# Layer-norm variance with eps out of the aggregation, one more unit by seven block products, and new instruction orders, in a two-layer long-convolution and SwiGLU kernel

## The chip, the cores and the metric

The kernel runs on one core of a Trainium2 chip. The core has a matrix engine (TensorE, PE in the profile, with its weight loads as PEld), a vector engine (VectorE, DVE), an activation engine (ScalarE, ACT), a general engine (GpSimd, POOL), a queue engine that here only issues DMAs (SyncE, SP), and 16 DMA engines. The metric is the device time of one execution in microseconds; lower is better. A fraction of a per cent is the scale of this case.

## The reference, cut to what matters

Two blocks, A and B, are applied twice, each as a residual on the layer-normed x of 2048 rows by 512 columns:

```python
def _layernorm(x, axis=-1, eps=1e-5):
    m = jnp.mean(x, axis=axis, keepdims=True)
    v = jnp.var(x, axis=axis, keepdims=True)
    return (x - m) / jnp.sqrt(v + eps)
...
x = A_q
x = x + _A_ref(_layernorm(x, axis=-1), A_k, A_v, A_shift_k, A_ssm_k, A_ssm_D)
x = x + _B_ref(_layernorm(x, axis=-1), B_w_gate, B_w_up, B_w_down)
x = x + _A_ref(_layernorm(x, axis=-1), A_k, A_v, A_shift_k, A_ssm_k, A_ssm_D)
x = x + _B_ref(_layernorm(x, axis=-1), B_w_gate, B_w_up, B_w_down)
```

Block A computes y = causal long convolution over the 2048 rows of (short convolution of k, times v) with the kernel ssm_k, plus a skip term, and returns q * y, where q is the normed x. The convolution doesn't depend on x, so y is computed once and used by both layers. Block B is (silu(x @ w_gate) * (x @ w_up)) @ w_down, with weights of 512 x 1792, 512 x 1792 and 1792 x 512.

## The kernel before, in words

**Tiling.** The rows are cut into 4 chunks (c = 0 to 3) of 512 rows, four rows to each of 128 partitions; a chunk has two halves (h = 0, 1) of two rows per partition. A *unit* (l, c, h) is block B of layer l on one half of one chunk, 256 rows. There are 16 units. The stretch ahead of a unit, `prologue(l, c, h)` (line 926), norms x (`apply_norm`), multiplies by y, adds to x, takes the second layer norm's statistics, writes the normed rows z, and turns them by a DMA transpose (line 940) into zT, which the unit's matmuls read.

**A unit** (`ffn`, line 1085) has 14 column tiles of 128 in groups of 4, 4, 4 and 2. For each group TensorE makes gate and up products into the four PSUM banks of ring "pf", ScalarE takes them out with Silu and a copy (lines 1072 and 1073, or 1132 and 1136), VectorE multiplies them, and in the row-wise form (`by_rows`) a DMA transpose (line 1081) turns the result. Then the down product (line 1159) accumulates over all 14 tiles: 28 matmuls of 512 columns per unit into two banks of ring "pd". ScalarE copies these two banks into `dn` (line 1201) and VectorE adds `dn` to x (line 1204).

**Seven products.** For units named in `STRASSEN` a number of groups takes another way: `seven` (line 1004) makes sums of blocks of the left operand on VectorE (tile `cb`, three instructions per group, lines 1013 to 1017) and does the 2x2 block product in seven products of 256 columns (line 1034) in place of eight, into four banks (two of "pd", two of "pc"). `weight_sums` (line 981) makes the sums of the blocks of w_down once, in five VectorE instructions (lines 994 and 998). `add_seven` (line 1038) takes four banks out and adds them to x in five VectorE instructions. Before, the four units of chunk 3 take it.

**The convolution** is done by Fourier blocks per chunk: transposes of ssm_k, forward products with ScalarE evacuation (line 466), butterflies on VectorE (lines 587 to 604), spectral products `product` (lines 700 to 714, 2048 elements per partition in the large ones) and the `inverse` of chunk c (line 728), whose rows y that chunk's prologue reads. The work of `conv(c)` must be over before unit (0, c, 0) starts.

**Layer-norm statistics** come in two ways. `ln_stats` (line 851) uses VectorE: `bn_stats` gives two triples (count, mean, sum of squares about it) for each row of 512, `bn_aggr` joins them into mean and variance, a third VectorE instruction (line 859) adds eps, and GpSimd raises the result to the power -0.5 (line 861). `ln_stats_act` (line 867) uses ScalarE: a copy with an accumulated sum, a mean, a square with an accumulated sum, and GpSimd's power (line 887).

**Order.** No scheduler decides. Every instruction group is recorded as an operation with its engine, a cost in microseconds and the operations that it depends on; the list `ORDER` holds for each operation its place in the one sequence, and each engine's queue is that sequence cut down to its own operations. `Plan.order` (line 200) also walks the sequence with the given costs to pick the slot of each ring buffer (the one that comes free first). All transposing DMAs stand in SP's single queue with the loads. An engine takes its queue strictly in order, so an instruction whose operand is late holds back all that stands behind it on its engine.

Of the kernel before, what the change touches and what calls it, by code (L numbers as in the profile page):

```python
# [9 lines left out]
P = 128  # L10
# [20 lines left out]
STRASSEN = {(0, 3, 0): 4, (0, 3, 1): 4, (1, 3, 0): 4, (1, 3, 1): 2}  # L31
# [88 lines left out]
]  # L120
R = 4

NS = 8
# [21 lines left out]
class Plan:  # L147
# [52 lines left out]
    def order(self, table):  # L200
# [14 lines left out]
        for o in seq:  # L215
# [26 lines left out]
            if o.late:  # L242
# [5 lines left out]
                elif gap[1] > o.start + 0.03:  # L248
                    settle(gap[0])
                    pend = None  # L250
# [1218 lines left out]
```

## Time and profile before

| what | value |
|---|---|
| median of three runs | 340.92 us (340.49 to 341.29) |
| the profiled execution | 340.95 us, of which 339.2 us span |
| granted TensorE clock | 0.998 |
| PE busy | 332.2 us |
| DVE busy | 305.4 us |
| ACT busy | 257.8 us |
| POOL busy | 41.1 us |
| SP | 150 of its DMA issues in the trace |

How to read it: the span runs from the first to the last profiled instruction; the execution's own time is 1.75 us longer. Busy time is the union of an engine's instructions; matmul durations overlap their successors, so the spacing of matmuls in the timeline (0.216 us for 512 columns, 0.109 us for 256) is what a matmul costs, not its mean duration. The same holds in smaller measure for VectorE: a 2048-element product lasts 1.22 us and the next instruction starts after 1.135 us. In the chain of waits a line is a start, a length, and the work that the chain ran through. A timeline line ends with the idle time ahead of the instruction and what ended it.

### The profile page before, as it was taken

The page shows a single profiled execution, that of the slowest core. Times are in us where ns is not written, and L with a number is a line of the kernel's source. Part 1 is how long each engine was busy: PE and PEld are TensorE (multiplying, and loading weights), DVE is VectorE, ACT ScalarE, POOL GpSimd, SP SyncE. Part 2 cuts the span into 40 slices and gives each one's busy share as a digit, 9 for nine tenths or more (in the row PEclk, how much of TensorE's full clock was granted, in tenths as well). Part 3 has the DMA queues.
Part 4 walks back from the last instruction along what each step waited for, and adds up shares of the span by engine and source line. Part 5 has one row for each costly group of instructions (what it writes and reads, how often), then busy time and mean ns, then how long its engine had stood idle before and what let it go on. Part 6 is the DMA issues. An engine that isn't in the chain of part 4 may idle for free.

```text
span 339.2 us, 5867 instructions
## 1 busy us (share of the span) xinstructions
PE 332.2 (98%) x2119; PEld 201.9 (60%) x2151; DVE 305.4 (90%) x552; ACT 257.8 (76%) x514; POOL 41.1 (12%) x46
## 2 busy tenths in 40 slices
PE   8999999999999999999999999999999999999996
PEld 6647864644454564654445555645445487867884
DVE  7999999999999999999999999999999866987464
ACT  6899999988987467877899994869575465657463
POOL 4010110303110400103010200111201000100000
PEclk9999999999999999999999999999999999999999
DMA  7999403312643458341323245431414140213201
GB/s 287 322 312 354 59 15 79 62 31 48 140 108 77 98 123 161 75 111 31 63 48 77 46 80 129 115 37 32 89 11 94 28 92 2 49 47 73 55 0 64
DMA packets 77992, 31.59 MB, mean 93 GB/s; under 512 B 69765, under 2 KB 75786, under 8 KB 77962
## 3 DMA queue, kind: packets, MB, share of 16 engines
q1 hardware_dynamic: 77808, 31.13, 39.5%
q8 instruction: 17, 0.28, 0.4%
q14 instruction: 13, 0.11, 0.1%
q10 hardware_dynamic: 154, 0.07, 0.1%
HBM read 12.33 MB, written 2.10 MB: 43 GB/s over the span
## 4 chain that ended last, share of the span: by engine, by line
PE 83%; ACT 6%; DVE 5%; DMA 4%; issue 1%; POOL 1%; SPq 0%; ACTq 0%
PE pf L358 51%; PE pd L1159 18%; PE ps L358 6%; PE ps L1034 6%; DMA zT<-z 2%; DMA kn<-in_A_k_dram 1%; PE ps L844 1%; ACT H L466 1%; ACT X L466 1%; PE ps L505 1%; DVE bnst L856 1%; DVE m L587 1%; ACT jk L881 1%; ACT jk L875 1%; ACT hs L534 1%
## 5 line engine op out<-in xcount | busy, mean ns | idle before, releaser
L358 PEld LDWEIGHTS <-zT 128*128 128x128 bf16 x528 | 51.4, 98 | 61.1 <-DMA zT<-z 1.4
L358 PE MATMUL pf<-wu_sb,zT 128*128 128x512 bf16 x258 | 64.8, 379 | 0.4
L358 PE MATMUL pf<-wg_sb,zT 128*128 128x512 bf16 x256 | 63.6, 379 | 0.6 <-DMA zT<-z 0.3
L1159 PE MATMUL pd<-wd_sb,sg 128*128 128x512 bf16 x217 | 53.4, 379 | 0.5 <-DMA sg<-hr 0.2
L861 POOL TENSOR_TENSOR rstd<-ve,nhalf 128x2 f32<-128x2 f32 x24 | 27.9, 1165 | 206.4 <-DVE ve L859 206.4
L1072 ACT ACTIVATE sg<-pf 128x512 bf16<-128x512 f32 x66 | 38.9, 605 | 11.9 <-PE pf L358 11.4
L1073 ACT CAST hr<-pf 128x512 bf16<-128x512 f32 x66 | 38.5, 591 | 11.8 <-PE pf L358 11.0
L358 PE MATMUL pf<-zT,wg_sb 128*128 128x256 bf16 x368 | 46.7, 273 | 0.1
L358 PE MATMUL pf<-zT,wu_sb 128*128 128x256 bf16 x368 | 45.9, 273 | 0.0
L358 PEld LDWEIGHTS <-wg_sb 128*128 128x128 bf16 x368 | 35.9, 98 | 8.4
L358 PEld LDWEIGHTS <-wu_sb 128*128 128x128 bf16 x368 | 36.0, 98 | 7.3
L1159 PEld LDWEIGHTS <-sg 128*128 128x128 bf16 x224 | 21.7, 98 | 24.2 <-DMA sg<-hr 0.9
L1132 ACT ACTIVATE sg<-pf 128x512 bf16<-128x512 f32 x46 | 27.5, 608 | 8.1 <-PE pf L358 8.0
L856 DVE BATCH_NORM_STATS2 bnst<-xc 128x6 f32<-128x512 bf16 x48 | 31.4, 684 | 0.5
L1136 ACT CAST ht<-pf 128x512 bf16<-128x512 f32 x46 | 26.7, 591 | 5.7 <-PE pf L358 5.5
L1159 PE MATMUL pd<-wd_sb,ht 128*128 128x512 bf16 (+1 forms) x125 | 30.2, 369 | 0.3
L1139 DVE TENSOR_TENSOR ht<-ht,sg 128x512 bf16<-128x512 bf16 (+1 forms) x31 | 16.9, 548 | 8.5 <-ACT ht L1136 5.0
L700 DVE TENSOR_TENSOR t<-X,G 128x2048 bf16<-128x2048 bf16 x18 | 21.9, 1217 | 0.0
L704 DVE TENSOR_TENSOR t<-X,G 128x2048 bf16<-128x2048 bf16 x18 | 21.9, 1217 | 0.0
L1201 ACT CAST dn<-pd 128x512 bf16<-128x512 f32 x24 | 14.1, 594 | 10.2 <-PE pd L1159 7.6
L466 ACT ACTIVATE X<-ps 128x512 bf16<-128x512 f32 x32 | 19.1, 613 | 3.5 <-PE ps L358 3.1
L1079 DVE TENSOR_TENSOR hr<-hr,sg 128x1024 bf16<-128x1024 bf16 x27 | 18.5, 685 | 2.4 <-ACT hr L1073 1.6
(139 smaller groups left out, 506.8 us busy)
## 6 DMA issues: line engine op xcount, KB each, us to landing
hn<-in_A_ssm_k_dram SPq DMA_DIRECT2D x4, 512.0 KB, 3.9
vt<-in_A_v_dram SPq DMA_DIRECT2D x4, 512.0 KB, 6.5
xc<-in_A_q_dram SPq DMA_DIRECT2D x4, 512.0 KB, 6.2
out_dram<-xc SPq DMA_DIRECT2D x15, 128.0 KB, 1.8
wg_sb<-in_B_w_gate_dram SPq DMA_DIRECT2D x1, 1792.0 KB
wu_sb<-in_B_w_up_dram SPq DMA_DIRECT2D x1, 1792.0 KB, 7.5
wd_sb<-in_B_w_down_dram SPq DMA_DIRECT2D x1, 1280.0 KB, 11.2
sg<-hr SPq DMA_TRANSPOSE x66, 2.5
```

Source lines behind the costliest of these rows:

```text
L358: nc.tensor.matmul(o, lhsT=lhsT, rhs=rhs, start=(n == 0), stop=(n == len(terms) - 1))
L466: add("ACT", act(D), lambda: nc.scalar.activation(out=view(), in_=ps.t[:], func=ACT.Copy, scale=scale), r=[ps], w=[(buf, keys)], conv=conv)
L700: dve(n * D, lambda t1=t1, part=part: nc.vector.tensor_mul(out=t1.t[:], in0=x.t[:, sl, 0, :], in1=g.t[:, sl, part, :]), [(x, key(slots, (0 ...
L704: dve(n * D, lambda t2=t2, part=part: nc.vector.tensor_mul(out=t2.t[:], in0=x.t[:, sl, 1, :], in1=g.t[:, sl, 1 - part, :]), [(x, key(slots ...
L856: add("DVE", 0.6, lambda st=st, i=i: nc.vector.bn_stats(out=st.t[:], in_=xs[c].t[:, i, :]), r=[(xs[c], (i,))], w=[st])
L861: add("POOL", pw, lambda: nc.gpsimd.tensor_tensor(out=rstd.t[:], in0=ve.t[:], in1=nhalf.t[:].to_broadcast((P, n)), op=ALU.pow), r=[ve, nha ...
L1034: nc.tensor.matmul(bank.t[:, half_ * C:(half_ + 1) * C], lhsT=lhsT(i), rhs=rhs(i), start=(first and i == 0 and half_ == 0), stop=(last and ...
L1072: add("ACT", act(D), lambda ps=ps, dst=dst, o=o, which=which: nc.scalar.activation(out=rows(dst, o), in_=ps.t[:], func=ACT.Silu) if which ...
L1073: out=rows(dst, o), in_=ps.t[:], func=ACT.Silu) if which == "g" else nc.scalar.copy(out=rows(dst, o), in_=ps.t[:]),
L1132: add("ACT", act(D), lambda ps=ps, o=o, sg=sg: nc.scalar.activation(out=sg.t[:, o:o + 2, :], in_=ps.t[:], func=ACT.Silu), r=[ps], w=[(sg, ...
L1136: add("ACT", act(D), lambda ps=ps, o=o, ht=ht: nc.scalar.copy(out=ht.t[:, o:o + 2, :], in_=ps.t[:]), r=[ps], w=[(ht, (o // 2,))], due=(uni ...
L1159: nc.tensor.matmul((pds[o] if not cs.start else pds[HP]).t[:, cs], lhsT=ht.tiles(q, o), rhs=wt["d"].t[:, ft, cs], start=(ft == std0 and no ...
```

## The change

1. `ln_stats` no longer adds eps in an instruction of its own. The statistics go into a constant buffer `bst` with six slots of nine numbers: two triples from `bn_stats`, and a third triple (0, 0, eps x 512) that two GpSimd memsets write once. `bn_aggr` joins all three, so that its variance already holds eps, and GpSimd's power reads it from `mv` with a stride. The 24 instructions of line 859 are gone.
2. Unit (1, 2, 1) is added to `STRASSEN` with all four groups. `weight_sums` is recorded ahead of that unit instead of ahead of (0, 3, 0).
3. The inverse of chunk 3 uses PSUM ring "pf" in place of "pc" (`I_RING`), since `seven` of (1, 2, 1) takes the "pc" banks.
4. For (1, 0, 0) the row sums come from the two copies of `dn` in unit (0, 0, 0), with an accumulator, and from the mean that the statistics before had given; one VectorE instruction joins them. Two ScalarE passes over x and one small ScalarE instruction go.
5. `ORDER` is a new list of 1744 places (1742 before). Costs and latencies of the walk and its rule for GpSimd are other numbers; they emit no instruction, and act through the slots alone. Rings: "st" 4 for 8, "mv" 9 for 6, "ve" 8 for 6.

```diff
-STRASSEN = {(0, 3, 0): 4, (0, 3, 1): 4, (1, 3, 0): 4, (1, 3, 1): 2}
+STRASSEN={(1,2,1):4,(0,3,0):4,(0,3,1):4,(1,3,0):4,(1,3,1):2}
+I_RING = lambda k: "pf" if k == 3 else "pc"
...
 ORDER = [
...
+BN_SLOTS = 6
...
+    bst = whole("bst", [P, BN_SLOTS, 9], F32)
...
-            ps = new("pc", "ps", [P, D], F32)
+            ps = new(I_RING(k), "ps", [P, D], F32)
...
+    def power(var, reads, n, cost):
+
+        rstd = new("rs", "rstd", [P, n], F32)
+        add("POOL", cost, lambda: nc.gpsimd.tensor_tensor(out=rstd.t[:], in0=var(), in1=nhalf.t[:].to_broadcast((P, n)), op=ALU.pow),
+            r=reads + [nhalf], w=[rstd])
+        return rstd
+
     def ln_stats(c, rows, pw=PW):
...
-            st = new("st", "bnst", [P, 6], F32)
-            add("DVE", 0.6, lambda st=st, i=i: nc.vector.bn_stats(out=st.t[:], in_=xs[c].t[:, i, :]), r=[(xs[c], (i,))], w=[st])
-            add("DVE", 0.09, lambda st=st, o=o: nc.vector.bn_aggr(out=mv.t[:, o, :], in_=st.t[:]), r=[st], w=[(mv, (o,))])
-        ve, rstd = new("ve", "ve", [P, n], F32), new("rs", "rstd", [P, n], F32)
-        add("DVE", 0.08, lambda: nc.vector.tensor_scalar(out=ve.t[:], in0=mv.t[:, :, 1], scalar1=LN_EPS, scalar2=None,
-                                                         op0=ALU.add), r=[mv], w=[ve])
-        add("POOL", pw, lambda: nc.gpsimd.tensor_tensor(out=rstd.t[:], in0=ve.t[:], in1=nhalf.t[:].to_broadcast((P, n)),
-                                                          op=ALU.pow), r=[ve, nhalf], w=[rstd])
-        return mv, rstd
+            st = plan.buf("bn", "bnst", lambda slot: bst.t[:, slot])
+            add("DVE", 0.6, lambda st=st, i=i: nc.vector.bn_stats(out=st.t[:, 0:6], in_=xs[c].t[:, i, :]), r=[(xs[c], (i,))], w=[st])
+            add("DVE", 0.09, lambda st=st, o=o: nc.vector.bn_aggr(out=mv.t[:, o, :], in_=st.t[:, 0:9]), r=[st, bst], w=[(mv, (o,))])
+        return mv, power(lambda: mv.t[:, :, 1], [mv], n, pw)
...
+            sm = None
+            if layer == 0 and ST1(1, c, h):
+                sm = new("st", "sm", [P, 2 * HP], F32, parts=2 * HP)
+                sums[1, c, h] = sm, means.pop((c, h))
...
+                    add("ACT", act(D) + 0.14, lambda o=o: nc.scalar.activation(
+                        out=dn.t[:, o, :], in_=pds[o].t[:], func=ACT.Copy, accum_out=sm.t[:, o:o + 1]), r=[pds[o]], w=[(dn, (o,)), (sm, (o,))],
+                        due=(unit, 1.0, 3.0, "h"))
...
+    add("POOL", 0.1, lambda: nc.gpsimd.memset(bst.t[:, :, 6:8], 0.0), w=[bst], due=-47)
+    add("POOL", 0.1, lambda: nc.gpsimd.memset(bst.t[:, :, 8:9], LN_EPS * D), w=[bst], due=-47)
...
     def run(unit):
+        if unit in STRASSEN and not ws:
+            weight_sums()
         ffn(unit)
...
     for c in range(NB):
-        if (0, c, 0) == min(STRASSEN):
-            weight_sums()
         run((0, c, 0))
```

More of the change, by code (lines that the diff above doesn't have):

```diff
@@ L183, in add @@
                         b.readers[k].append(o)
-        o.two = eng == "DVE" and not any(b.ring in ("pf", "pc", "pd") or b.name == "bnst" for b in o.bufs)
-        o.late = 0
-        if eng == "POOL" and any(b.name == "rstd" for b in o.bufs):
-            o.late = 2 if any(q.eng == "ACT" and any(b.name == "ve" for b in q.bufs) for q in o.preds) else 4
+        o.two = eng == "DVE" and not any(b.ring in ("pf", "pc", "pd") or b.ring == "bn" for b in o.bufs)
+        o.late = int(eng == "POOL" and any(b.name == "rstd" for b in o.bufs))
         for b in o.bufs:
@@ L206, in order @@
         place, todo, free_at = {}, {}, {}
-        pend, gap, last = None, (0.0, 0.0), 0.0
+        pend, vec = None, []
         def settle(g):
-            pend.end = max(pend.start + pend.cost, max(g, pend.start) + pend.cost - 0.13)
+            pend.end = max(pend.start + pend.cost, g + pend.cost - 0.08)
             t["POOL"] = max(t["POOL"], pend.end)
@@ L216, in order @@
             if pend is not None and (o.eng == "POOL" or pend in o.preds):
-                settle(t["DVE"])
+                settle(0.0)
                 pend = None
@@ L229, in order @@
                     own[place[b]] = b
+            o.end = o.start + o.cost
             if o.eng == "DVE":
-                last = o.start
-                if pend is not None and pend.late == 4 and o.start + o.cost > pend.start:
-                    settle(0.0 if o.start >= pend.start - 0.02 else o.start + o.cost)
+                vec.append(o)
+                if pend is not None and (o.start >= pend.start + 0.08 or (o.two and o.end > pend.start)):
+                    settle(0.0 if o.start >= pend.start + 0.08 else o.end)
                     pend = None
-                g = (t["DVE"], o.start if o.two else o.start + o.cost)
-                if g[1] > g[0] + 0.05:
-                    gap = g
-                    if pend is not None and g[1] > pend.start + 0.03:
-                        settle(g[0])
-                        pend = None
-            o.end = o.start + o.cost
-            if o.late:
-                pend, t["POOL"] = o, o.end
-                if o.late == 4:
-                    if t["DVE"] > o.start:
-                        settle(t["DVE"] if last < o.start else 0.0)
-                        pend = None
-                elif gap[1] > o.start + 0.03:
-                    settle(gap[0])
+            if o.late:
+                pend, n = o, len(vec) - 1
+                while n >= 0 and vec[n].start >= o.start + 0.08:
+                    n -= 1
+                if n >= 0 and vec[n].two and vec[n].end > o.start:
+                    settle(vec[n].end)
                     pend = None
-            t[o.eng] = max(t[o.eng], o.end) if o.late else o.end
+                elif n < len(vec) - 1:
+                    settle(0.0)
+                    pend = None
+            t[o.eng] = max(t[o.eng], o.end)
             for b in o.bufs:
@@ L257, in order @@
         if pend is not None:
-            settle(t["DVE"])
+            settle(0.0)
         return seq, place, {o: (o.start, o.end) for o in self.ops}
@@ L388, in load_h @@
             return o
-        return add(eng, 0.55, lambda: q.dma_start(out=hn[b].t[:], in_=h3[:, :, b * L:(b + 1) * L]), w=[hn[b]], lat=(LH0, 9.0)[b] if b < 2 else 13.0 if b == 2 else 6.0, due=due, after=after)
+        return add(eng, 0.55, lambda: q.dma_start(out=hn[b].t[:], in_=h3[:, :, b * L:(b + 1) * L]), w=[hn[b]], lat=(LH0, 9.0)[b] if b < 2 else 13.0 if b == 2 else 5.5, due=due, after=after)
     def load_k(b, due=None, after=()):
@@ L400, in load_k @@
         kT[b] = new("s8" if b == 1 else "k", "kTb", [P, KD, PADL + L])
-        return add("SP", 5.5 if b == 1 else 2.2, lambda: nc.sync.dma_start_transpose(out=kT[b].t[:], in_=k3[b * L - PADL:(b + 1) * L]),
-            w=[kT[b]], lat=3.7 if b == 1 else 11.5 if b == 2 else 8.0, due=due, after=after)
+        return add("SP", (2.6, 9.0, 4.4)[b - 1], lambda: nc.sync.dma_start_transpose(out=kT[b].t[:], in_=k3[b * L - PADL:(b + 1) * L]),
+            w=[kT[b]], lat=3.7 if b == 1 else 2.6, due=due, after=after)
     def transpose_k(b, ring, engs):
@@ L659, in shift_mul_t @@
             add("SP", 1.25, lambda r=r: nc.sync.dma_start_transpose(
-                out=ks.t[:, 0, r], in_=a.t[:, 0, r]), r=[(a, range(KD))], w=[(c, (r,))], lat=4.0, conv=True)
+                out=ks.t[:, 0, r], in_=a.t[:, 0, r]), r=[(a, range(KD))], w=[(c, (r,))], lat=2.0, conv=True)
         for h in range(2):
@@ L876, in ln_stats_act @@
                     out=jk.t[:], in_=xs[c].t[:, i, :], func=ACT.Copy, accum_out=sm.t[:, o:o + 1]), r=[(xs[c], (i,))], w=[jk, (sm, (o,))], after=after)
-        nm = new("mv", "nm", [P, n], F32)
-        add("ACT", TINY, lambda: nc.scalar.mul(out=nm.t[:], in_=sm.t[:, 0:n], mul=-1.0 / D), r=[(sm, range(n))], w=[nm])
+            add("ACT", TINY, lambda: nc.scalar.mul(out=nm.t[:], in_=sm.t[:, 0:n], mul=-1.0 / D), r=[(sm, range(n))], w=[nm])
+        else:
+            at, op = (lambda: prev.t[:, :, 0], ALU.subtract) if prev.name == "mv" else (lambda: prev.t[:], ALU.add)
+            add("DVE", 0.08, lambda: nc.vector.scalar_tensor_tensor(out=nm.t[:], in0=sm.t[:, 0:n], scalar=-1.0 / D, in1=at(), op0=ALU.mult, op1=op),
+                r=[(sm, range(n)), prev], w=[nm])
         for o, i in enumerate(rows):
@@ L883, in ln_stats_act @@
                 r=[(xs[c], (i,)), nm], w=[jk, (sm, (n + o,))])
-        ve, rstd = new("ve", "ve", [P, n], F32), new("rs", "rstd", [P, n], F32)
+        ve = new("ve", "ve", [P, n], F32)
         add("ACT", TINY, lambda: nc.scalar.activation(out=ve.t[:], in_=sm.t[:, n:2 * n], func=ACT.Identity, scale=1.0 / D, bias=eps.t[:]),
             r=[(sm, range(n, 2 * n)), eps], w=[ve])
-        add("POOL", PWA, lambda: nc.gpsimd.tensor_tensor(out=rstd.t[:], in0=ve.t[:], in1=nhalf.t[:].to_broadcast((P, n)),
-                                                          op=ALU.pow), r=[ve, nhalf], w=[rstd])
-        return nm, rstd
+        return nm, power(lambda: ve.t[:], [ve], n, PWA)
     def shift_of(st, n, due=None):
@@ L1183, in ffn @@
             sm = None
-            if layer == 0 and ST1(1, c, h):
-                sm = sums[1, c, h] = new("st", "sm", [P, 2 * HP], F32, parts=2 * HP)
             for o in range(HP):
@@ L1199, in ffn @@
             dn = new("dn", "dn", [P, HP, D], parts=HP)
+            sm = None
+            if layer == 0 and ST1(1, c, h):
+                sm = new("st", "sm", [P, 2 * HP], F32, parts=2 * HP)
+                sums[1, c, h] = sm, means.pop((c, h))
             for o in range(HP):
[L1201 to L1202 removed]
+                if sm is None:
+                    add("ACT", act(D), lambda o=o: nc.scalar.copy(out=dn.t[:, o, :], in_=pds[o].t[:]), r=[pds[o]], w=[(dn, (o,))],
+                        due=(unit, 1.0, 3.0, "h"))
+                else:
+                    add("ACT", act(D) + 0.14, lambda o=o: nc.scalar.activation(
+                        out=dn.t[:, o, :], in_=pds[o].t[:], func=ACT.Copy, accum_out=sm.t[:, o:o + 1]), r=[pds[o]], w=[(dn, (o,)), (sm, (o,))],
+                        due=(unit, 1.0, 3.0, "h"))
             sl = span(rows)
```

23 lines of the change are left out of this document (12 added, 11 removed), and 130 rows, old and new, of the table ORDER.

## The prediction

> **What bounds the kernel now.** I read the page's busy times first, then its chain shares, then the windows and the timeline at the places where TensorE stands still. Page, busy times and chain shares by engine:
>
> ```profile
> span 339.2 us, 5867 instructions
> PE 332.2 (98%) x2119; PEld 201.9 (60%) x2151; DVE 305.4 (90%) x552; ACT 257.8 (76%) x514; POOL 41.1 (12%) x46
> PE 83%; ACT 6%; DVE 5%; DMA 4%; issue 1%; POOL 1%; SPq 0%; ACTq 0%
> ```
>
> TensorE is busy for 98% and carries 83% of the chain: less matrix work shortens the span, unless the operands come too late for it. The windows (length, then PE, PEld, DVE, ACT, POOL busy, clock, DMA share, GB/s) say where they could:
>
> ```profile
> 200.00:220.00 20.00, 19.89 (x124) 12.12 (x124) 19.24 (x28) 13.83 (x28) 1.00 (x1) 1.00 0.46 114
> 220.00:240.00 20.00, 19.90 (x100) 9.77 (x101) 19.29 (x33) 17.13 (x40) 4.14 (x3) 1.00 0.28 46
> 260.00:280.00 20.00, 19.91 (x127) 12.42 (x128) 15.82 (x33) 10.12 (x18) 1.85 (x3) 1.00 0.31 62
> ```
>
> To 256 us VectorE is as full as TensorE and only just ahead; from 260 us it has four idle microseconds in twenty. The chain of waits (start, length, work) shows the prices of matrix work and the two visible stops:
>
> ```profile
> 48.89 3.45 PE pd L1159 x16
> ...
> 85.99 4.19 DMA zT<-z
> 90.22 6.22 PE pf L358 x28
> ...
> 241.21 3.00 DMA zT<-z
> 244.25 6.22 PE pf L358 x28
> ...
> 295.28 5.35 PE ps L1034 x49
> ```
>
> A 512-column matmul costs 3.45/16 = 0.216 us, a 256-column one of the seven products 5.35/49 = 0.109. The stop at 244.25 is where the change works; its timeline:
>
> ```profile
> 238.97 1.22 DVE L700 TENSOR_TENSOR t<-X,G 128x2048 bf16<-128x2048 bf16 x1
> 239.03 2.35 POOL L887 TENSOR_TENSOR rstd<-ve,nhalf 128x2 f32<-128x2 f32 x2 [7.75 <-ACT ve L885]
> 240.77 0.41 DVE L911 TENSOR_SCALAR z<-xc,nm,rstd 128x512 bf16<-128x512 bf16 x1 [0.58 <-POOL rstd L887]
> 241.21 2.98 SPq L940 DMA_TRANSPOSE zT<-z  x2
> 244.25 0.60 PE L358 MATMUL pf<-wg_sb,zT 128*128 128x512 bf16 x2 [0.28 <-DMA zT<-z]
> ```
>
> GpSimd's power starts 0.06 us into a VectorE product, lasts 1.70 us (the group line joins two powers, 2.35 together; the second, at 240.71, takes 0.68), VectorE idles 0.58 us for it, the transpose lands 3.00 us after issue, and TensorE has been idle for about 0.46 us (its spacing; the group line says 0.28). All 32 powers divide alike: 0.68 to 0.80 us without a VectorE product beside them, 1.5 to 1.74 when begun inside one.
>
> **The change part by part.** *Seven products for (1,2,1).* 28 down matmuls go (28 x 0.2155 = 6.04 us), 49 of 256 columns come (49 x 0.109 = 5.34): **-0.70 us** of TensorE. There are 21 more weight loads of 98 ns (groups of line 1034), 2.06 us; PEld at 60% hides them, as it does in the 49 matmuls above, which already carry a load each. By "TensorE: Matmul & The Clock Gate", section "Back-to-back issue gap", of the Trainium skill, load and matmul together set a sustained spacing of about 131 ns at 512 columns and 81 at 128; interpolating to an estimated 98 at 256, the part would cost 28 x 0.131 = 3.67 against 49 x 0.098 = 4.80, a loss of 1.1 us. The trace's 216 and 109 ns disagree with it.
>
> VectorE gains 12 `cb` instructions (3.17 us at 0.336, 0.20 and 0.19) and `add_seven` for a plain add (+1.38). ScalarE drops two `dn` copies and makes four others for the sums, here nothing: it is 50 to 70% busy there.
>
> *Eps in the aggregation.* 24 instructions of line 859 go. Each occupies VectorE for 0.077 us (start to next start; it lasts 0.166): -1.85 us. The 48 aggregations read nine numbers for six: from `bn_stats` (0.603 for 512) and aggregation (0.0995 for 6) about 1 ns each, +0.14; bounds 0 and 48 x 0.05. The power of each norm can start some 0.2 us sooner. POOL has two memsets more (0.09 for 128x1 at 5.48), long before use.
>
> *Sums of (1,0,0).* Two passes of ScalarE go (0.62 each), two copies gain an accumulator read (0.14 each), VectorE gains one small instruction (0.09). The z transposes there (the chain's 85.99, 4.19 us long, against 2.45 usually) can start some 2.0 us sooner, TensorE asks 1.3 sooner. The load of v for chunk 2, issued at 85.36 right in front of them, moves three transposes of line 1081 ahead in SP's queue, so it may slow those instead. Gain 0 to 0.39 (the stops of 0.12 at 83.45 and 0.27 at 90.22); a loss of one slow transpose, 4.19 - 2.45 = 1.7, less their slack, is the other end. I count 0: what is won or lost this early meets VectorE's chain below, which then sets the time.
>
> *VectorE in sum:* -1.85 + 3.17 + 1.38 + 0.09 + 0.14 = +2.9 us. Up to z of (0,3,0) its queue is 1.1 us shorter; from there to the statistics of (1,3,0) it goes from 17.4 to 20.2 us, in a stretch of 25 us (260.98 to 285.95). That hides it; without this cover it costs up to 2.8.
>
> *Ring "pf" for the inverse of chunk 3.* Its four rows stand there between gate and up tiles. Price if a bank is late: one ScalarE evacuation, 0.48; in the trace TensorE waits on none. I take 0; ends 0 and 0.48.
>
> *The new order around (1,2,1).* SP issues the same 152 DMAs. From chunk 2 of layer 1 on no z transpose has a load newly in front of it; some change sides with transposes of line 1081, of about 1.2 us issue each, and one that is late would hold z's for that long. I take 0, since z is what comes last there now. In the head and at chunk 1 loads of ssm_k, v, x and k change places too, where TensorE has no stop now but the named ones; 0 again, ends -0.4 and 1.7 as above. I follow one chain, with durations from before:
>
> 1. x add of (0,2,1), now at 227.12 after 0.54 us of VectorE idling for ScalarE: VectorE comes with 0.49 us more queued ahead, TensorE's tile 0.21 us of work sooner. So 226.6 to 227.1.
> 2. To the x add of the prologue of (1,2,1): 6.65 us before (227.12 to 233.77), less one line 859: 6.57. So 233.2 to 233.7.
> 3. ScalarE's statistics: power 4.57 us after the add's end (234.46 to 239.03), less one evacuation of 0.48, moved behind: add start + 0.69 + 4.09 = + 4.78.
> 4. VectorE meanwhile: add and five 1024-element instructions (6 x 0.602), slack 0.1, and two products (1.135 each) before z; the 0.336 of line 1076 that stood between them moves behind. The second starts at + 4.84, so the power falls 0.06 us **ahead** of it and should take 0.69, ending at + 5.47. z starts at + 5.97: 239.15 to 239.65 (was 240.77).
> 5. + 0.44 and an ordinary 2.45: zT lands 242.05 to 242.55. TensorE asks at 242.1 to 242.5 (244.25 less 1.3 us of work sooner, the 0.46 and perhaps 0.4 of older waits): a wait of 0 to 0.2 for 0.46.
> 6. TensorE now has row 1 of chunk 3's inverse 3.0 us of work sooner, right behind; it needs the rotations that stand 12.2 us of VectorE slots after z, 12.7 real (9.98 were needed for 9.48 from 242.90 on). They end at 251.85 to 252.35, TensorE is there at 251.2 to 251.6: **a new wait of 0.3 to 0.8**. It had 1.5 us to spare.
> 7. z of (0,3,0) is 17.7 us of slots behind; zT lands at 260.3 to 261.0, TensorE wants it at 260.6 to 261.1 (4.3 us of work sooner than before): 0 to 0.2.
>
> Steps 5 to 7 share one lag: a wait at one shortens the next. Together TensorE stands 0.1 us less to 0.35 more than now. I take **+0.15**, a little over the middle, since step 6 has less to spare than 5.
>
> Sum against the profiled execution (340.95: span 339.2 and 1.75 around it, 0.03 over the median): 340.95 - 0.70 + 0.15 = **340.4**. Own range: 340.0 (waits -0.25) to 340.85 (+0.6).
>
> **The rivals.**
> - *The power falls inside the second product.* Step 4 leaves 0.06 us. If ScalarE is a hair later, the rows of 1.53 to 1.74 us apply, and z comes about 0.7 later, and with it steps 5 to 7: 341.0 to 341.3. For it: the narrow margin, and that it is what the trace shows now. Against: the aggregation's shorter path to other powers moves ScalarE's work forward.
> - *VectorE bounds the stretch behind z of (0,3,0)* (the other side). The seven products of (1,2,1) and (0,3,0) need 24 `cb` in 20.2 us of slots, among weight sums of 1.00 each. It decides once that queue is over 1.5 us behind, since the first `cb` groups have only 0.2 to 1 us to spare; then TensorE waits on `cb` or `ht` there, and of the 2.8 us more, 1.0 to 2.8 show: 341.4 to 343, likeliest 342. For it: some tiles are asked 2 to 5 us earlier. Against: 4.2 us idle in 260 to 280.
> - *All waits go, none comes.* 0.39 at 82 to 90 and 0.46 at 244, and ScalarE's early end lets step 6 hold: 340.95 - 0.70 - 0.85 = 339.4, with part of it 339.7. For it: the chain's order is the same with each norm 0.2 us quicker, which over several norms in a row could give VectorE the 0.5 that step 6 lacks. Against: VectorE idles under 5 us in 225, so little is there to be won.
> - *The seven products do not pay*: the 21 added loads show, 2.06 us, 342.3. Against: the row of 5.35 us for 49. By the skill's spacing, above, it would be 342.2.
>
> **How the numbers follow.** About 0.2% is what a measurement of this kernel can tell from no change: 340.24 to 341.60. Main case 0.42 (0.10 of it under 340.24, 0.32 within); power inside the product 0.15 (0.09 within, 0.06 over, where other waits add); VectorE bound 0.18 (0.02 within, 0.16 over); all waits gone 0.20 (faster); no pay 0.05 (slower). Faster 0.30, same 0.43, slower 0.27. Range 339.5 to 342.2: it leaves out half of the last rival, the upper third of VectorE's, and a quarter of the waits-gone case, some 0.15.
>
> **What would show it.** PE 512-column matmuls 28 fewer and 49 more of 256 at 0.109; line 859 gone and aggregations of about 0.1; z of (1,2,1) near 239.4, its power 0.7 and just ahead of a product; the stop before its first matmul under 0.2; a stop of 0.3 to 0.8 some 9 us later, before the inverse's second row, put down to a rotation; none on `cb` afterwards. I am wrong if the first big stop lies elsewhere: in the head, where order changes too, on `cb`, or on an inverse bank in ring "pf".

## The result, and the profile after

The change makes the kernel slower: 344.98 us in the median (343.83 to 345.91, six runs) against 341.12 (340.49 to 341.96), a ratio of 1.011 with a 95% interval of 1.0086 to 1.0134. The forecast was 340.4, range 339.5 to 342.2. The profiled execution of the changed kernel is the fastest of its six: 343.83 us, span 342.0.

The page of the changed kernel, span, busy times and the chain's shares by engine:

```profile
span 342.0 us, 5917 instructions
PE 332.0 (97%) x2140; PEld 203.8 (60%) x2172; DVE 306.6 (90%) x545; ACT 257.0 (75%) x513; POOL 37.1 (11%) x48
PE 43%; DVE 38%; ACT 6%; issue 5%; DMA 4%; SPq 2%; POOL 2%; DVEq 0%; ACTq 0%; POOLq 0%
```

TensorE's busy time is hardly less, but it carries 43% of the chain where it carried 83%: between its stretches of work the chain now runs back through VectorE and through transposes. (Line numbers have moved: L353, L1083 and L941 are the lines 358, 1081 and 940 of before. `hr` is a group's product of gate and up, `sg` its transpose, which the down product reads.) The chain itself, its three longest DMA pieces and one of the seven products:

```profile
79.23 4.34 DMA sg<-hr
...
128.20 5.56 DMA zT<-z
...
220.34 4.36 DMA sg<-hr
...
298.18 5.35 PE ps L1036 x49
```

The last line is the block product at its old price, 0.109 us each. The others are transposes that took 4.3 to 5.6 us from issue to landing, where an ordinary one takes 2.4 to 2.5. SP's queue and TensorE around the second, then SP's queue around the first:

```profile
126.27 1.26 SPq L941 DMA_TRANSPOSE zT<-z  x1
127.65 0.51 SPq L429 DMA_DIRECT2D xc<-in_A_q_dram  x1
128.20 3.17 SPq L941 DMA_TRANSPOSE zT<-z  x1
```

```profile
131.70 1.24 PE L353 MATMUL pf<-wg_sb,zT 128*128 128x512 bf16 x5
133.81 1.04 PE L353 MATMUL pf<-wg_sb,zT 128*128 128x512 bf16 x4 [0.86 <-DMA zT<-z]
```

```profile
77.38 1.19 SPq L1083 DMA_TRANSPOSE sg<-hr  x1
78.61 0.58 SPq L425 DMA_DIRECT2D vt<-in_A_v_dram  x1
79.23 5.19 SPq L1083 DMA_TRANSPOSE sg<-hr  x3
```

In the kernel before, the load of v stood behind four such transposes, and that of x behind both z transposes:

```profile
79.22 6.09 SPq L1081 DMA_TRANSPOSE sg<-hr  x4
85.36 0.58 SPq L429 DMA_DIRECT2D vt<-in_A_v_dram  x1
...
124.03 2.50 SPq L940 DMA_TRANSPOSE zT<-z  x2
126.64 0.51 SPq L433 DMA_DIRECT2D xc<-in_A_q_dram  x1
```

A load of x, half a megabyte, now stands between the two z transposes of one unit; the second is issued 0.04 us after it, takes 3.17 us to issue and 5.56 to land, and TensorE stands still. The load of v stands likewise ahead of the transpose of 79.23.

Measured by the spacing of matmuls (time between two starts beyond the 0.2155 us that a 512-column matmul takes, which is some 0.16 more than the bracket gives), TensorE's time went as follows, profile against profile, 2.87 us in all. A stop is named by the start of the last matmul ahead of it:

| where | us |
|---|---|
| 28 matmuls of 512 columns less, 49 of 256 more | -0.70 |
| head, up to 32 us: stops 2.48 before, 1.81 after (0.57 of it at 29.0, new, on VectorE's vt) | -0.67 |
| the stops before at 82.9, 89.7 and 243.6 are gone | -1.06 |
| new stops at 82.4 and 132.6, on transposes issued right behind a load (0.99, 1.03) | +2.02 |
| new stops at 59.3 and 223.6, on transposes that landed in 4.0 and 4.4 us with no load near, beside the 16 KB transfers told of below (0.56, 0.89) | +1.45 |
| new stops at 111.9, 208.9, 230.6 and 254.9, on an sg issued late, on VectorE's ht, on ScalarE's copies and on a rotation (0.72, 0.23, 0.27, 0.54) | +1.76 |
| sum (the rest to 2.87 is in spacings under 0.1) | +2.80 |

The other runs of the changed kernel are up to 2.1 us longer than this one; where their stops are isn't known.

Two theories were tested, and a rival. **L**: the loads' new places in SP's queue make the transposes behind them late. **F**: a transpose is also late when it meets one of 17 transfers of 16 KB that the page lists as a queue of its own (window 79 to 84 of the changed kernel, DMA view):

```profile
q1 hardware_dynamic: 1438, 0.83, 68.3%
q8 instruction: 1, 0.02, 1.8%
```

They bring TensorE's instructions: there are 17 for 4,344 instructions (2,172 weight loads and a matmul for each, of which the trace lacks 32), and from one to the next TensorE starts 198 to 267 instructions, some 250 in the mean. So fewer instructions in the head move them later in the work. **O**, the rival: VectorE's new order makes everything late, and the transposes are only where it is seen.

### The profile page after: what moved, and what is told of

It is laid out like the page before. It is cut to its first block, busy times and chain, and to the rows that moved or that the text cites. A ratio compares the mean times of both kernels' runs of the same rounds, so it can differ in the third digit from the quotient of the medians.

```text
span 342.0 us, 5917 instructions
## 1 busy us (share of the span) xinstructions
PE 332.0 (97%) x2140; PEld 203.8 (60%) x2172; DVE 306.6 (90%) x545; ACT 257.0 (75%) x513; POOL 37.1 (11%) x48
## 4 chain that ended last, share of the span: by engine, by line
PE 43%; DVE 38%; ACT 6%; issue 5%; DMA 4%; SPq 2%; POOL 2%; DVEq 0%; ACTq 0%; POOLq 0%
PE pf L353 24%; PE ps L1036 7%; PE pd L1161 7%; PE ps L353 4%; DVE m L583 3%; DVE t L700 3%; DVE t L696 3%; DVE bst L859 3%; DMA sg<-hr 3%; DVE t L708 2%; DVE hr L1081 2%; DVE G L624 2%; DVE Z L710 2%; DMA zT<-z 2%; POOL rstd L850 2%
## 5 line engine op out<-in xcount | busy, mean ns | idle before, releaser
L353 PEld LDWEIGHTS <-zT 128*128 128x128 bf16 x528 | 51.6, 98 | 60.2 <-DMA zT<-z 1.6
L353 PE MATMUL pf<-wg_sb,zT 128*128 128x512 bf16 x259 | 64.9, 379 | 1.2 <-DMA zT<-z 0.9
L353 PE MATMUL pf<-wu_sb,zT 128*128 128x512 bf16 x255 | 64.5, 379 | 0.5
L1161 PE MATMUL pd<-wd_sb,sg 128*128 128x512 bf16 x193 | 47.9, 379 | 2.5 <-DMA sg<-hr 2.1
L850 POOL TENSOR_TENSOR rstd<-mv,nhalf 128x2 f32<-128x2 f32 x24 | 23.9, 997 | 218.1 <-DVE mv L860 218.1
L353 PE MATMUL pf<-zT,wu_sb 128*128 128x256 bf16 x368 | 45.9, 273 | 0.1
L1074 ACT ACTIVATE sg<-pf 128x512 bf16<-128x512 f32 x66 | 38.7, 602 | 9.6 <-PE pf L353 6.2
L353 PE MATMUL pf<-zT,wg_sb 128*128 128x256 bf16 x368 | 45.7, 273 | 0.1
L353 PEld LDWEIGHTS <-wu_sb 128*128 128x128 bf16 x368 | 36.0, 98 | 8.1
L353 PEld LDWEIGHTS <-wg_sb 128*128 128x128 bf16 x368 | 36.0, 98 | 7.4 <-issue 0.7
L1134 ACT ACTIVATE sg<-pf 128x512 bf16<-128x512 f32 x46 | 26.6, 601 | 14.9 <-PE pf L353 12.3
L1161 PEld LDWEIGHTS <-sg 128*128 128x128 bf16 x200 | 19.3, 98 | 25.0 <-DMA sg<-hr 3.6
L859 DVE BATCH_NORM_STATS2 bst<-xc 128x6 f32<-128x512 bf16 x48 | 31.6, 682 | 0.6
L1161 PE MATMUL pd<-wd_sb,ht 128*128 128x512 bf16 (+1 forms) x122 | 28.6, 369 | 0.2
L1206 ACT CAST dn<-pd 128x512 bf16<-128x512 f32 x20 | 11.7, 591 | 11.0 <-PE pd L1161 10.9
L1161 PEld LDWEIGHTS <-ht 128*128 128x128 bf16 x126 | 12.2, 98 | 12.6 <-DVE ht L1141 0.6
```

The lines of the kernel that those rows point to most:

```text
L353: nc.tensor.matmul(o, lhsT=lhsT, rhs=rhs, start=(n == 0), stop=(n == len(terms) - 1))
L850: add("POOL", cost, lambda: nc.gpsimd.tensor_tensor(out=rstd.t[:], in0=var(), in1=nhalf.t[:].to_broadcast((P, n)), op=ALU.pow), r=reads + ...
L859: add("DVE", 0.6, lambda st=st, i=i: nc.vector.bn_stats(out=st.t[:, 0:6], in_=xs[c].t[:, i, :]), r=[(xs[c], (i,))], w=[st])
L1074: add("ACT", act(D), lambda ps=ps, dst=dst, o=o, which=which: nc.scalar.activation(out=rows(dst, o), in_=ps.t[:], func=ACT.Silu) if which ...
L1134: add("ACT", act(D), lambda ps=ps, o=o, sg=sg: nc.scalar.activation(out=sg.t[:, o:o + 2, :], in_=ps.t[:], func=ACT.Silu), r=[ps], w=[(sg, ...
L1161: nc.tensor.matmul((pds[o] if not cs.start else pds[HP]).t[:, cs], lhsT=ht.tiles(q, o), rhs=wt["d"].t[:, ft, cs], start=(ft == std0 and no ...
```

## The experiments

**Moving the 16 KB transfers by fewer instructions in the head.** In both kernels TensorE is kept busy by 33 warm-up matmuls, and as many weight loads, before its first data. The edit of the first run (the other two have -20):

```diff
+SHIFT = [-12]
-                    warm(*max(free, key=nxt.get), n)
+                    warm(*max(free, key=nxt.get), n + SHIFT.pop() if SHIFT else n)
```

> The changed kernel with 12 fewer of the 33 warm-up matmuls that fill TensorE before its first data, nothing else. Theory F (fetch): the 17 transfers of 16 KB on the instruction queue come once per some 256 TensorE instructions and hold up the transpose that they meet, to 3.3 to 4.4 us from issue to landing for 2.4 to 2.5; 24 instructions fewer in the head move each transfer about 2 us later in the work, away from the transposes that TensorE waited for at 59.3, 82.4 and 223.6 us (0.56 + 0.99 + 0.89) and partly from those behind the stops at 111.9 and 132.6 (0.72 + 1.03). F expects 341.0 to 342.5 us against about 344.5 for the changed kernel, those three stops gone or under 0.2. Theory O (order): the transposes are late because VectorE and the loads ahead of them are, whatever is fetched. O expects 344 to 345.5, the same stops. Fewer warm-ups by themselves: the first matmuls on data wait for a load landing at 4.2 to 4.7 us in both kernels, so 0, at most 0.3 slower if they run slowly at first.

> The changed kernel with 20 fewer warm-ups: the same transfers some 3.5 us later than in the changed kernel. F: the stops at 59, 82, 132 and 224 go or shrink, but the transfers now meet the transposes issued at about 110, 203 and 275 us, which have 0.0, 0.3 and 0.1 us to spare: new stops of 1 to 1.7 us near 111 and 204, and 1.5 in VectorE's block sums near 276. Total 343 to 345.5, not told from the changed kernel by its time, but by its places. O: 344 to 345.5, stops where they were.

> The kernel before with 20 fewer warm-ups, order untouched. F: the transfers leave the places where the kernel before could bear them and meet transposes issued at about 59, 84, 201, 223, 273 and 290 us, with 0.3 to 0.6 us of TensorE's time lost at the first four and 1.6 in VectorE at the last two, part of it covered: 342 to 344 us against 341.1. O: 340.8 to 341.4, no new stop.

Measured: 347.79 us (ratio to before 1.021, 1.0186 to 1.0235) for 12 fewer, 345.65 (1.0151, 1.0122 to 1.0179) for 20 fewer, and 343.35 (1.0071, 1.0048 to 1.0095) for the kernel before with 20 fewer. The head was misjudged in all three: with TensorE idle there its first matmuls ran at half speed for longer (0.427 us for 512 columns; the full clock was granted at 7.4, 10.0 and 10.0 us, against 3.5 and 3.6 without the edit), and its first down product came 1.4, 2.6 and 2.1 us later than without the edit (41.86 and 43.08 us for 40.49; 43.17 for 41.12), which is nearly all that the third run lost. The times therefore decide nothing; the places do. With 20 fewer, TensorE's timeline near the two places that F had named (about 111 and 204):

```profile
115.46 0.82 PE L1162 MATMUL pd<-wd_sb,sg 128*128 128x512 bf16 x3 [1.29 <-DMA sg<-hr]
```

```profile
208.94 1.04 PE L1162 MATMUL pd<-wd_sb,sg 128*128 128x512 bf16 x4 [1.41 <-DMA sg<-hr]
```

By spacing these stops are 1.46 and 1.57 us (F had 1.7 and 1.4 for the transposes behind them), the first grown from 0.72, the second new; those of 59, 132 and 224 are gone and that of 82 has 0.72 for 0.99, as F said and O did not. Of F's third new place, VectorE's block sums, 0.63 shows (at 282.2) for 1.5. With 12 fewer the stops of 59 and 224 are gone too, but that of 82 grew from 0.99 to 2.54: there F failed, for the transpose behind the load of v now met the transfer of 84.05 and landed in 5.62; and that of 112 grew from 0.72 to 1.48. In the kernel before, the stops at 82.9 and 89.7 went, that at 243.6 shrank from 0.44 to 0.15, and two of the four that F had named came (0.61 at 65.0, 0.61 at 228.6): against the profile before, 0.45 us worse after the head. So the transfers have a say in *which* transposes are late, but moving them mostly exchanged stops.

**Part 1 alone, on the kernel before.** `ln_stats` with the third triple, line 859 gone, the old order without those 24 places:

```diff
+            st = plan.buf("bn", "bnst", lambda slot: bst.t[:, slot])
...
-            add("DVE", 0.09, lambda st=st, o=o: nc.vector.bn_aggr(out=mv.t[:, o, :], in_=st.t[:]), r=[st], w=[(mv, (o,))])
+            add("DVE", 0.09, lambda st=st, o=o: nc.vector.bn_aggr(out=mv.t[:, o, :], in_=st.t[:, 0:9]), r=[st, bst], w=[(mv, (o,))])
-        add("DVE", 0.08, lambda: nc.vector.tensor_scalar(out=ve.t[:], in0=mv.t[:, :, 1], scalar1=LN_EPS, scalar2=None,
...
```

> The kernel before with part 1 of the change alone: eps as a third triple of the aggregation, 24 VectorE instructions of line 859 gone, two memsets on GpSimd, all other instructions in their old order (TensorE's 4304 unchanged, so the instruction transfers stay at the same places in the work). Both theories: VectorE 1.7 us shorter, each norm 0.2 us sooner, but TensorE sets the time and its stops before are 0.34 at 82.9, 0.27 at 89.7 and 0.44 at 243.6: 340.3 to 341.1 against 341.1. If 341.5 or more, part 1 itself carries part of the loss (a power falling into a product where it did not).

Measured 340.69 us, ratio 0.9998 (0.9984 to 1.0012): no loss, and no gain that can be told from none. Part 1 is no part of the loss.

**The two loads, out of the changed kernel and into the kernel before.** Only places in `ORDER` differ (names for the two loads and their new neighbours):

```diff
 # changed kernel
-ORDER[load_v(2)] = between sg(1,0,0) and sg(1,0,0)
-ORDER[load_x(2)] = between zT(0,1,1) and zT(0,1,1)
+ORDER[load_v(2)] = behind the fourth hs of chunk 2
+ORDER[load_x(2)] = behind both zT(0,1,1)
 # kernel before
-ORDER[load_v(2)] = ahead of both zT(1,0,1)
-ORDER[load_x(2)] = behind both zT(0,1,1)
+ORDER[load_v(2)] = behind the first sg(1,0,0)
+ORDER[load_x(2)] = between zT(0,1,1) and zT(0,1,1)
```

> The changed kernel with two loads moved in SP's queue: that of v for chunk 2 from between the transposes of line 1083 (issued at 78.61) to right behind the one of line 638 at 70.79, and that of x for chunk 2 from between the two z transposes (127.65) to behind both. TensorE's instructions are untouched. Theory L (loads): a transpose issued right behind a load that still runs takes 3.8 to 5.6 us to land, as at 79.23 and 128.20; the stops at 82.4 (0.99) and 132.6 (1.03) go to 0 to 0.3, and with them 1.4 to 2.0 us: 342.9 to 343.6 against 345.0. Theory F alone (the 16 KB transfers at 79.34 and 128.54 are enough): the first keeps 0.5 or more, the second goes since that transpose starts 0.55 earlier with 2 us to spare: 343.6 to 344.4. Theory O (VectorE's order): 344.5 to 345.5, the time comes back as waits on VectorE.

> The kernel before with the same two loads put where the change puts them: v for chunk 2 behind the first of the four transposes of line 1081 issued from 79.22 on, x for chunk 2 between the two z transposes of 124.03 and 125.27. L: the next transposes of line 1081 land 1 to 2 us later (1.4 us to spare), the stop at 82.9 grows from 0.34 to 1 to 2, that at 89.7 (0.27) goes; the second z transpose of 125.27 lands 1.3 to 3.1 later with 2.0 to spare, a stop of 0 to 1.1: 341.6 to 343.3 against 341.1. O: 340.8 to 341.4.

Measured: the changed kernel fell to 343.28 us (ratio to before 1.0064, 1.0041 to 1.0086), 1.70 less, and the kernel before rose to 343.72 (1.0079, 1.0054 to 1.0104), 2.6 more. L holds in both directions (the second run came 0.4 us above L's range), and O's time doesn't come back. TensorE and SP in the kernel before with the new places:

```profile
125.85 0.41 SPq L456 DMA_DIRECT2D xc<-in_A_q_dram  x1
126.31 1.19 SPq L963 DMA_TRANSPOSE zT<-z  x1
```

```profile
131.94 1.90 PE L381 MATMUL pf<-wu_sb,zT 128*128 128x512 bf16 x8 [1.55 <-DMA zT<-z]
```

```profile
85.02 1.04 PE L1182 MATMUL pd<-wd_sb,sg 128*128 128x512 bf16 x4 [0.83 <-DMA sg<-hr]
```

Its chain gives 5.58 us for that zT, which met a 16 KB transfer too (at 129.86, just after the load had landed). The two stops are 1.71 and 1.00 by spacing, of the same sort as in the changed kernel; the expected sizes were 0 to 1.1 and 1 to 2. In the changed kernel with the loads moved both stops are gone, and the chain's share of TensorE is back from 43% to 63%:

```profile
span 340.7 us, 5917 instructions
PE 63%; DVE 21%; ACT 6%; issue 4%; DMA 3%; POOL 1%; SPq 1%; DVEq 0%; POOLq 0%; ACTq 0%
```

The two transposes still met their 16 KB transfers and landed in 4.01 and 3.48 us, but nothing waited for them. What is left above the kernel before are the stops at 59.7 (0.52), 111.2 (1.09), 222.3 and 223.6 (0.88 together), 253.6 (0.54), and those of the new order at 29.3, 207.5 and 229.3 (0.57, 0.25, 0.27).

**The seven products taken out of (1,2,1) again**, in the changed kernel (`ORDER` follows: the places of the dropped instructions go, and the plain add and the copies take new ones):

```diff
-STRASSEN={(1,2,1):4,(0,3,0):4,(0,3,1):4,(1,3,0):4,(1,3,1):2}
+STRASSEN={(0,3,0):4,(0,3,1):4,(1,3,0):4,(1,3,1):2}
```

> The changed kernel with unit (1,2,1) taken out of the seven products again: 28 down matmuls of 512 columns and a plain add stand where the 49 of 256 stood; weight sums, ring pf for the inverse and all other places stay, except the add of (1,2,0), which goes ahead of the new copies. Both theories: TensorE has 0.70 us more work, VectorE 3.2 + 1.4 less. If the seven products gave their 0.70: 345.4 to 346. If VectorE's 4.6 us more after 240 us cost what they gained: 344.2 to 345.2, with the stop at 254.9 unchanged, since it stands ahead of the block sums. If below 344, the seven products were themselves part of the loss.

Measured 344.61 us (ratio to before 1.0105, 1.0084 to 1.0127), in the middle of the second range. The time alone would say that seven products are worth nothing or less. The two traces say otherwise: from the first matmul of the last inverse to the end the changed kernel takes 342.05 - 254.65 = 87.40 us, this one 342.15 - 254.06 = 88.09: 0.69 more, the 0.70 forecast. What it gains lies ahead: the stop at 132.6 is absent in its profile, where the zT behind the load of x landed in 4.43 us for 5.56, with the same queue. So the products pay where they stand, and a late transpose elsewhere weighs more.

**A search for a version without late transposes.** Warm-ups can be folded into wider ones, so that the head streams as many columns with fewer instructions:

```diff
-        t = psp.tile([P, P], F32, name="wm", tag=f"{ring}{slot}")
-        for _ in range(n):
-            nc.tensor.matmul(t[:], lhsT=ones, rhs=ones, start=True, stop=True)
+        t = psp.tile([P, 2 * P], F32, name="wm", tag=f"{ring}{slot}")
+        for m in [2 * P] * k + [P] * (n - 2 * k):
+            nc.tensor.matmul(t[:, 0:m], lhsT=ones, rhs=two[:, 0:m], start=True, stop=True)
```

> The kernel before with part 1 alone and six pairs of warm-ups made one each of 256 columns, so that TensorE streams as many columns in the head with 12 instructions fewer. In the run of part 1 alone TensorE had one stop after 30 us, 0.83 at 245.3, where a z transpose issued at 242.11 met the 16 KB transfer of 243.92, 1.8 us into it. F: the transfer comes 12 instructions, some 1.0 us, later in the work, when the transpose has landed; the stop goes, and no other transpose on TensorE's path with less than 1.7 us to spare is met: 339.7 to 340.3 against 341.1 before and 340.7 for part 1. O: 340.5 to 340.9.

> The changed kernel with twelve pairs of warm-ups made one each of 256 columns: 24 TensorE instructions fewer, as in the run with 12 fewer, but as many columns in the head, so its first matmuls should not run slowly (0 to 0.3 us in the head). Loads where the change puts them. F: the 16 KB transfers come some 2 us later in the work; the stop at 59.3 (0.56) goes, that at 223.6 falls from 0.89 to 0.3, that at 111.9 loses 0.5 of 0.72; those behind the loads stay in part (82.4: 0.4 or more, since a transpose behind a load alone takes 3.8; 132.6: 0 to 1): 342.3 to 343.7 against 345.0. If 344.5 or more, the transfers are not what those three stops hang on, or their new places cost as much.

> Both repairs: the two loads moved as in the run that gave 343.3, and the twelve wide warm-ups. F and L together: of the stops left there, 59.7 (0.52) goes, 111.2 (1.09) falls by 0.5, 222.3 and 223.6 (0.88 together) fall to 0.3; those of the head at 29.3 (0.57) and of the rotation at 253.6 (0.54) stay: 341.4 to 342.2, still above the kernel before by what these two and the rest of 111 cost. If the gains of the two repairs do not add (343 or more), the chain behind TensorE is VectorE's after all.

Measured: 340.73 us (0.9987, 0.9970 to 1.0004) for the first, in O's range and not in F's. The stop at 245 is gone as F expected, but one of 0.66 stands at 89.1 in its place, behind the load of v; no gain. The second, 345.52 (1.013, 1.0109 to 1.0152), is a miss of F, beyond the 0.9 us that the head lost here too (first down product at 41.41): the stops of 59 and 224 are gone, that of 82 is 2.30 (the transpose behind the load of v now meets the transfer of 82.68 and lands in 5.39), 113.7 has 1.04, that of 132 still has 0.75, and 207.5 has 0.88. The third, 342.38 (1.0037, 1.0020 to 1.0054), lies 0.2 above its range. It shows that the stop of 82 needed the load: with the load away and the transfers about where the second run had them there is none. In the medians 0.9 is gained over the run with moved loads, though the head lost 0.8; left are 111.6 (1.34), 205.0 (0.60), 150.2 (0.32), 253.9 (0.52), and 30.1 and 229.7 (0.57, 0.27).

**The load of v earlier, on the kernel before with part 1 and the six wide warm-ups.** The load goes behind the two z transposes that land at 72.2, where SP has nothing to issue for 6 us:

```diff
-ORDER[load_v(2)] = ahead of both zT(1,0,1)
+ORDER[load_v(2)] = behind both zT(1,0,0)
```

> The kernel before with part 1, the six wide warm-ups, and the load of v for chunk 2 moved from right ahead of the z transposes (85.4 in before) to behind the two z transposes that end at 72.7, where SP then has nothing for 6 us. Left of TensorE's stops after 30 us in the run without this move: one of 0.66 at 89.1, behind that load. L: it goes, no other comes, and the runs whose transposes the load met now and then go too: 339.7 to 340.4 against 341.1 before. If 340.6 or more, something else than stops on late transposes sets what is left.

Measured 339.92 us, ratio 0.9972 (0.9960 to 0.9984): faster than both kernels, by a third of a per cent. Its page, span and the chain's shares by engine:

```profile
span 337.8 us, 5866 instructions
PE 97%; ACT 2%; issue 0%
```

After 30 us no matmul starts late by more than a lost record's spacing, and the chain is TensorE.

> The same kernel as the last one (part 1, load of v early: no TensorE stop after 30 us, 339.9 us), with ten more pairs of warm-ups folded into wider ones: same columns in the head, 20 TensorE instructions fewer, no load, order or dependence touched. F: the 16 KB transfers come some 1.7 us later in the work; of the transposes that they then meet, the one issued at 83.95 has 0.7 us to spare and that at 58.82 1.4, so there come stops of about 1.0 us near 86.5 to 87 and 0.3 near 62, and one of 1.7 in VectorE at 272, where it has 4 us idle: 340.8 to 341.4 against 341.1 before, ratio 0.999 to 1.001. O: no new stop, 339.7 to 340.1, ratio 0.997.

Here the same fold was made wider still, five warm-ups of 512 columns and one of 256 in all. Measured 340.32 us (339.60 to 344.0), ratio 0.9975 (0.9963 to 0.9988). The profiled execution was the longest of them: in the head a load of k landed at 7.87 us for 5.57, TensorE stood still for 2.52 us, and its granted clock was then halved for 3.41 us, which touches neither theory but makes all that follows 3.7 us later. F failed on the main stop: the one of 1.0 near 87 did not come. There were late transposes there (issued at 86.04, landed 4.11 us later), but TensorE didn't wait for them. Only that near 62 came, 0.67 at 66.3. The ratio expected by F, 0.999 to 1.001, lies outside the interval; O's 0.997 lies in it. With the loads out of the way this kernel bore the transfers, but for one stop, in both sets of places that were tried.

**What a late transpose is.** The 1,164 transposes from on-chip memory to on-chip memory with a known landing in all fourteen traces, sorted by what overlapped their flight. Left out are one of `inv` per run in the head, which landed 11 to 14 us after its issue among the first loads. A load whose own landing isn't known counts as running for 4 us:

| beside the transpose | count | issue to landing, us | over 2.7 us |
|---|---|---|---|
| nothing | 860 | 2.29 to 2.53, median 2.43 | 0 |
| a 16 KB instruction transfer | 162 | 2.33 to 4.42, median 3.23 | 106 |
| an 8 KB one (the other instruction queue) | 87 | 2.34 to 3.29, median 2.44 | 8 |
| a load still running that was issued ahead | 40 | 2.39 to 4.24, median 3.60 | 25 |
| that load and a 16 KB transfer | 15 | 2.50 to 5.62, median 4.34 | 14 |

None was over 2.53 us without a load or an instruction transfer beside it. Beside a load alone it went by the time between the two issues: the 20 transposes issued 0.5 to 1.0 us after the load took 3.75 to 4.24 us, the five issued 1.9 to 2.3 us after it 3.05 to 3.46, and the 15 from 2.8 us on 2.39 to 2.60. That a load just ahead is a cause was shown by moving the loads both ways; for the instruction transfers it rests on this table and on stops that went or came as they moved. Why the overlap delays a transpose (a shared engine, ring or port) was not tried and stays open.

## Why the prediction was wrong

**Step by step.**
- *Seven products, -0.70*: right (0.69 between two traces, 0.109 each). The 21 loads of weights are hidden.
- *Eps, nothing or a little*: right in what it is worth (0.9998, no loss); an aggregation of nine numbers lasts 186 ns for 172, 14 ns more, inside its bounds and above the 3 ns taken.
- *Sums of (1,0,0) and ring "pf"*: the stop at 89.7 is gone, and no stop of the changed kernel was put down to an inverse's bank. Neither was tried by itself.
- *Order around (1,2,1), steps 1 to 7*: the structure held. The x add of (0,2,1) came at 230.10, 3 us late from the stops ahead; from there to z it took 12.92 us, forecast 12.54. Step 4's margin of 0.06 us went the other way, as in the first rival. (The rule that it used, that all 32 powers last 0.68 to 0.80 or 1.5 to 1.74 us, misread the trace: eight others of before lasted 0.81 to 1.35, and one 4.13. SP's DMAs are 150 in both traces, not 152.) The power and z of the changed kernel:

```profile
241.22 1.21 DVE L700 TENSOR_TENSOR t<-X,G 128x2048 bf16<-128x2048 bf16 x1
241.35 2.29 POOL L850 TENSOR_TENSOR rstd<-ve,nhalf 128x2 f32<-128x2 f32 x2 [7.35 <-ACT ve L887]
243.02 0.41 DVE L911 TENSOR_SCALAR z<-xc,nm,rstd 128x512 bf16<-128x512 bf16 x1 [0.59 <-POOL rstd L850]
```

  The power starts 0.13 us inside the product and lasts until z. Even so, the stop at z is gone (step 5), and the new one on a rotation came where step 6 had it, 0.54 us for 0.3 to 0.8:

```profile
255.62 0.60 PE L353 MATMUL ps<-Z,inv 128*128 128x512 bf16 x2 [0.37 <-DVE Z L600]
```

- *VectorE as the bound behind (0,3,0)*: did not come; VectorE stood idle for 2.97 us there, waiting for an sg, and TensorE didn't wait for `cb`.
- **The step that failed** is the price of the new places of loads in SP's queue, which the sum put at 0. For the load of v the text had seen that it "moves three transposes of line 1081 ahead" and "may slow those instead", with one slow transpose, 1.7 us less slack, as the other end, and then counted 0, since what is lost early would meet VectorE's chain at (1,2,1). For the loads in the head and at chunk 1, that of x among them, it took "0 again, ends -0.4 and 1.7 as above". Measured: 2.02 for the two loads in the profile, 1.70 in the median when they are moved back, 2.6 when the kernel before gets them. A slow transpose's price of 1.7 was of the right kind and low (4.34 and 5.56 us for 2.45, so 1.9 and 3.1), and before had it in a line shown: zT at 85.99, 4.19 us, right behind a load. But two loads had moved, and each paid it where TensorE had little time to spare. The argument that an early loss is absorbed was wrong: VectorE's chain began 3 us later with everything else, for its x add waits for TensorE's product.
- The second gap: for the slow transpose of before without a load ahead (3.0 us at 241.21, beside an 8 KB transfer of 242.40) step 5 simply put an ordinary 2.45, and did not ask what had slowed it. Transposes beside a 16 KB transfer recur every 250 or so TensorE instructions, and the new order left less room for that at 59 and 224. Worth 1.45 here, by the profile alone.
- The third: 1.76 us of new stops belong to the new order of VectorE and ScalarE. Step 6 had forecast one (0.54 of it); those at 111.9, 208.9 and 230.6, and 0.57 at 29.0 in the head, it had at nothing. So O is refuted as the cause of the stops behind the loads, but not for this part: no run moved VectorE's order, and with both repairs the kernel was still 1.3 us slower than before.

The prediction's sign of being wrong did come: the first big stops lie elsewhere, from 29.0 and 59.3 on. No rival had this mechanism; those that were to end on the slower side put the loss at the power, behind z of (0,3,0), or on the added weight loads.

By the Trainium skill, "Runtime: NRT & Kernel Launch", section "Instruction fetch mechanics", instructions are fetched in blocks of 16 KiB, 256 of them, over a DMA queue of the engine's own, and the cost is mostly hidden. The traces agree on blocks and count (17 of 16 KB for 4,344). For TensorE itself it is hidden: in the run with v moved early no matmul after 30 us starts late at any of them. For transposes in flight it isn't: 106 of 162 came late.

## What to carry to other kernels

Read every move of a load in a DMA queue as a price on the first transpose issued right behind it, here 1.3 to 1.8 us, and up to 3.2 with an instruction transfer beside it, and on a second some 2 us behind it (0.6 to 1.0); from 2.8 us on there was none. Set it against their spare time one by one, and put loads where the queue then has nothing to issue for as long. Beside an instruction transfer a transpose was late by 0.8 us in the median and by 2.0 at most, so an order that leaves less room than that is paid for now and then. A part that saves work can be right to a hundredth of a microsecond and be buried by a neighbour: cut the trace at a common instruction before judging it by the total.

## What the runs showed of the hardware beyond that

A TensorE stop can cost more than itself. With 12 warm-ups fewer the stop of 2.54 us at 83.3 was followed by matmuls 0.427 us apart until 89.4, 1.6 us more. Windows of that run (length, then busy times of PE, PEld, DVE, ACT and POOL, clock, DMA share, GB/s):

```profile
85.00:90.00 5.00, 3.91 (x11) 1.49 (x12) 2.22 (x6) 0.39 (x1) 1.19 (x1) 0.66 0.41 82
90.00:95.00 5.00, 5.00 (x25) 2.25 (x23) 3.75 (x7) 4.95 (x10) 0.00 (x0) 1.00 0.00 2
```

The granted clock was halved for 3.41 us. The same came after the stop of 2.52 us in the head of the last run. With twelve wide warm-ups a stop of 2.30 us at nearly the same place as the first left it at 1.00. These are three stops; that their length alone decides isn't shown.
